# Turning attention probabilities by a DMA transpose of float16 halves instead of PE transposes, from the fifteenth unit on

## The chip, the core and the metric

The kernel runs on one core of one Trainium2 chip. The time is the device time of one execution in microseconds (us). Engines are named as in the profile: PE is TensorE (matmuls), PEld its weight loads, DVE is VectorE, ACT is ScalarE, POOL is GpSimd, SP is SyncE, whose queue issues all of this kernel's DMAs. Each engine runs its instructions in the order in which they stand; an instruction that waits holds everything behind it on the same engine.

## What is computed

Attention inside chunks of 64 positions, then two feed-forward stages. Cut to what matters:

```python
# batch 8, heads 8, sequence 576 in 9 chunks of 64, head size 64
scores = scale * np.matmul(q_c, k_c.transpose(0, 1, 2, 4, 3))
scores = scores - np.max(scores, axis=-1, keepdims=True)
attn = np.exp(scores)
attn = attn / (np.sum(attn, axis=-1, keepdims=True) + 1e-09)
out = np.matmul(attn, v_c)
# then, with x = out as (8, 576, 512):
xn = (x - mu) / np.sqrt(var + 1e-06) * g_ln
x = x + np.maximum(xn @ w_ch1, 0.0) @ w_ch2        # 512 -> 2048 -> 512
# then a gated second stage (moe2) with w_in, a product over the sequence with w_sg, and w_out
```

All of it is float32 in the reference. The kernel forms the large products from float16 halves (a high part and the rest), three matmuls for each.

## The kernel before

The 4608 rows are 36 tiles of 128 rows. `attention(t)`, t from 0 to 35, is one **unit**: one tile, two chunks side by side on the partitions, eight heads. Its steps are scores on PE (`qk`, 16 float32 matmuls of 64x64 into the two banks of `pair`), the row maximum `mx` and the subtraction into `pm` on DVE, the exponential in place on ACT, four 128x128 transposes of `pm` on PE (`pt_`, float32, against `ident`, back into the score half of `pair`), the row sums `sm` and their reciprocals on DVE, a copy of the turned probabilities from `pair` to `pt` on ACT, the product with the values on PE (`pv_`, 16 matmuls of 64x64), and the division into `x` on DVE. From t = 10 (`JOIN`) on, `pv_` of unit t and `qk` of unit t + 1 stand directly behind each other on PE, as one step. `norm` then makes the normalised tile: statistics on DVE, 1/sqrt on POOL, `xn` on DVE, the high half on ACT and the rest on POOL into `hl`, and one DMA transpose `xT<-hl`, issued by SP, of both halves (128 partitions by 1024 float16, eight 128x128 pieces). Two tiles make a block b of 256 rows; `xT` has two buffers, `x` six, `pt` and `pair` one.

The middle of the program is a loop over blocks 4 to 17. For each block and each of eight column groups j, `ff1p` makes 24 matmuls of 256 columns (L677) into a bank, ACT and DVE make sums and halves of it (L692, L699 to L701, L704, L705), and `ff2p`, two groups later, makes 21 matmuls of 256 columns (L729) into `acc`. At the end of a block DVE and ACT bring `acc` back (L752, L757), POOL adds it to x (L762), and SP writes x to `x2d`. Beside this loop run the attention units of the block after next, and, early in it, the preparation of the second stage's weights (`prep`, `halve`: L435, L847, L904 to L910), of which six loads of 1 MB (`raw`, one buffer) are a part. The second stage follows, from a plan of its own.

What sets the order is a planner (`Plan`): every step is entered with an engine, a length in ns, what it reads and writes, a priority and a `lat`, the time that the planner lets pass from the end of the step to the start of a step on another engine that uses it. The planner runs through these lengths and writes out each engine's instructions in the order in which it could start them. Attention units have priority 10 t, the feed-forward steps over 1000, weight preparation 9000 (lower goes first). For t from 12 on, an attention step has `lat` 1000, and two ACT steps have `far`, 3000. So the order is fixed when the program is built; how long a step waits on the chip is another matter.

Of the kernel before, what the change touches and what calls it, by code (L numbers as in the profile page):

```python
# [9 lines left out]
F16 = mybir.dt.float16  # L10
F32 = mybir.dt.float32
# [3 lines left out]
AF = mybir.ActivationFunctionType  # L15
ALU = mybir.AluOpType
# [7 lines left out]
TUNE = dict(  # L24
    a=[-2457, -2682, -1491, -1906, -601, 1801, 3166, 1800],
    w=[2691, 1942, 2717, 1334, 683, 2853, 1967, 684],
    w2=[2022, 3167, 2350, 2598, -1558, -90, 1802, 1496],
    an=[101, 0, 1229, 131, 0, 119, -1201, 1189],
    wb=[112, -57, 0, 128, -102, -1215, 134, -121],
    lo=[0, 0, 0, 0, 1, 0, 0, 1],  # L30
    wl=[0, 0, 1, 1, 0, 0, 1, 0],
    wc=[0, 1, 1, 1, 1, 0, 0, 1],
    wa=[1, 1, 1, 0, 1, 1, 1, 0],
    wm=[0, 0, 0, 1, 0, 1, 1, 0],
    xn=[0, 1, 0, 0, 1, 1, 0, 1],
    g=[150, 12000, 200, 400, 150],
    f=[685, -1559, 2691],
# [105 lines left out]
def fused_kernel(ctx: ExitStack, tc, qkv, w1, w2, g1, w_in, w_out, wsgt, wsgs, g2, b_sg, out):  # L143
    nc = tc.nc
    PSUM = bass.MemoryType.PSUM
    P = 128
# [32 lines left out]
    ident = small.tile([P, P], F32, name="ident")  # L179
# [31 lines left out]
    op = plan.op  # L211
# [59 lines left out]
    def palloc(tag, bufs, shape, dt, pool=None):  # L271
        return plan.buf(tag, bufs, lambda: (pool or pools["att"][1]).tile(shape, dt, tag=tag, name=tag, bufs=bufs))
# [2 lines left out]
    xT_t = {}  # L275
    started = {}
    JOIN = 2 * B0 + 2

    def scores(t, o):

        a = palloc("qk", 2, [P, 2, 512], F32) if t < JOIN else palloc("qkl", 1, [P, 2, 512], F32)
        src = qkv[t].rearrange("p (a f) -> p a f", a=3)
        o("SP", 1700, lambda: nc.sync.dma_start(out=a.t, in_=src[:, 0:2]), wr=[a], lat=2200 if t < JOIN else 4000)
        s2 = pair[t % 2 if t < 6 else 1]

        def qk():
            for hp in range(4):
                for r in (slice(0, 64), slice(64, 128)):
                    for c in range(2):
                        k = hp * 128 + c * 64  # L290
                        nc.tensor.matmul(
                            s2[64 * c:64 * c + 64, r.start // 64, hp * 64:hp * 64 + 64],
                            lhsT=a.t[r, 0, k:k + 64],
                            rhs=a.t[r, 1, k:k + 64],
                            start=True,
                            stop=True,
                        )

        started[t] = a, qk

    def attention(t):
        n = t % 2 if t < 6 else 1
        s2, ks = pair[n], f"pair{n}"
        kp = ks if t < JOIN else "pairv"
        pr = TUNE['a'][t] if t < 8 else 10 * t
        lat = TUNE['g'][2] if t < 8 else 300 if t < JOIN else 600 if t < JOIN + 2 else 1000
        far = dict(lat=1500 if t < JOIN + 2 else 3000) if t >= JOIN else {}
        z = 1

        def o(eng, ns, fn, **k):  # L310
            ns = FAST.get((eng, ns), ns)
            op(eng, ns, fn, prio=k.pop("prio", pr), lat=k.pop("lat", lat), **k)

        if t not in started:
            scores(t, o)
            a, qk = started[t]
            o("PE", 1260 * z, qk, rd=[a], wr=[ks])
        v = palloc("v", 2, [P, 512], F32) if t < JOIN else palloc("vl", 1, [P, 512], F32)
        o("SP", 730, lambda: nc.sync.dma_start(out=v.t, in_=qkv[t].rearrange("p (a f) -> p a f", a=3)[:, 2]), wr=[v], lat=2200)
        mx = palloc("mx", 2, [P, 2, 4, 1], F32)  # L320
        pm = palloc("pm", 2, [P, 4, 2, 64], F32)
        sm = palloc("sm", 2, [P, 4, 2, 1], F32)
        rd = palloc("rd", 2, [P, 4, 2, 1], F32)
        pt = palloc("pt", 1, [P, 4, 128], F32)
        if t < 2:
            x = plan.buf(f"x{t}", 1, lambda: stage.tile([P, 512], F32, name=f"x{t}"))
        else:
            x = palloc("x", 6, [P, 512], F32, px)
        sv = s2[:, :, 0:256].rearrange("p a (h k) -> p a h k", h=4)
        pv = s2[:, :, 256:512].rearrange("p a (h d) -> p a h d", h=4)  # L330

        def pt_():
            for hp in range(4):
                nc.tensor.transpose(
                    s2[:, hp // 2, hp % 2 * 128:hp % 2 * 128 + 128], pm.t[:, hp].rearrange("p a k -> p (a k)"), ident
                )

        def pv_():
            for hp in range(4):
                for r in (slice(0, 64), slice(64, 128)):  # L340
                    for c in range(2):
                        k = c * 256 + hp * 64
                        nc.tensor.matmul(
                            s2[64 * c:64 * c + 64, r.start // 64, 256 + hp * 64:256 + hp * 64 + 64],
                            lhsT=pt.t[r, hp, 64 * c:64 * c + 64],
                            rhs=v.t[r, k:k + 64],
                            start=True,
                            stop=True,
                        )

        def rd_():
            nc.vector.tensor_scalar_add(sm.t, sm.t, 1e-9)
            nc.vector.reciprocal(rd.t, sm.t)

        o("DVE", 600, lambda: nc.vector.tensor_reduce(out=mx.t, in_=sv, axis=AX.X, op=ALU.max), rd=[ks], wr=[mx])
        o("DVE", 600, lambda: nc.vector.tensor_tensor(
            out=pm.t.rearrange("p h a k -> p a h k"), in0=sv, in1=mx.t.to_broadcast([P, 2, 4, 64]), op=ALU.subtract
        ), rd=[ks, mx], wr=[pm])
        o("ACT", 520, lambda: nc.scalar.activation(out=pm.t, in_=pm.t, func=AF.Exp, scale=0.125), wr=[pm], **far)
        o("PE", 850, pt_, rd=[pm, "ident"], wr=[ks, kp] if t >= JOIN else [ks])  # L360
        o("DVE", 600, lambda: nc.vector.tensor_reduce(out=sm.t, in_=pm.t, axis=AX.X, op=ALU.add), rd=[pm], wr=[sm])
        o("DVE", 330, rd_, rd=[sm], wr=[sm, rd])
        o("ACT", 480, lambda: nc.scalar.activation(
            out=pt.t.rearrange("p (a h) q -> p a h q", a=2),
            in_=s2[:, :, 0:256].rearrange("p a (h q) -> p a h q", h=2),
            func=AF.Copy,
        ), rd=[ks], wr=[pt], **far)
        if t < JOIN or t + 1 == NT:
            o("PE", 1260 * z, pv_, rd=[pt, v], wr=[kp])
        else:  # L370
            scores(t + 1, o)
            a_, qk_ = started[t + 1]
            o("PE", 1260, lambda: (pv_(), qk_()), rd=[pt, v, a_], wr=[kp, ks])
        o("DVE", 600, lambda: nc.vector.tensor_tensor(
            out=x.t.rearrange("p (h a d) -> p a h d", h=4, a=2),
            in0=pv,
            in1=rd.t.rearrange("p h a o -> p a h o").to_broadcast([P, 2, 4, 64]),
            op=ALU.mult,
        ), rd=[kp, rd], wr=[x])
        after = pr + (TUNE['an'][t] if t < 8 else 0)  # L380
        norm(t, x, lambda *a, **k: o(*a, prio=after, **k))
# [399 lines left out]

    bW = {"top": Buf("topB", None)}

    ATT = [f"{n}{k}" for n in ("qk", "v", "mx", "pm", "sm", "rd", "bs", "mv", "rs", "hl") for k in range(2)] + ["pt", "xn", "qkl", "vl", "u0", "u1"]
    w2s = {}

    def open_sums():
# [217 lines left out]
    def first_x2():  # L1005
        pr = 9500
        op("DVE", 100, lambda: absmax(redg[:, 0:1], x2mx[:, 0:GT]), rd=[f"x2mx{i}" for i in range(GT)], wr=["redg"], prio=pr, lat=3000)
        par(e2g[:, 0:1], redg[:, 0:1], ["redg"], ["x2e"], pr, True)
        op("DVE", 600, lambda: x2_cols(0, 1), rd=["win_s"], wr=["x2e", "sx0"], prio=pr)
        for p in range(5):  # L1010
            x2_make(plan, 0, p, pr)

    tops = [Buf(f"top{i}", None) for i in range(2)]
    with tc.manual_schedule():
# [10 lines left out]
        for i, b in enumerate(tops):  # L1025
# [4 lines left out]
        op("SP", 60, lambda: nc.sync.dma_start(out=g1s, in_=g1), wr=["g1s"], prio=3, lat=2200)  # L1030
        make_w1(0)
        attention(1)
        make_w1(1)
        attention(2)
# [3 lines left out]
            out=bb, in_=b_sg.rearrange("(o s) -> o s", o=1).partition_broadcast(P)[:, 0, :]  # L1038
# [38 lines left out]
        used += [f"late{n}{b}{k}" for n in "hl" for b in "ab" for k in range(16)]  # L1077
        op(None, 0, open_sums, wr=used + ATT + ["sums"], prio=0)
        for f in range(NF):
# [23 lines left out]
        for b, j in todo:  # L1103
            ff2p(b, j)
        op(None, 0, open_x2, rd=["xsL"], wr=["x2L"] + ATT, prio=0)
        first_x2()
# [19 lines left out]
        def fixed(tag, bufs, shape, dt=F32):  # L1126
            tiles[tag] = [room[-1].tile(shape, dt, name=f"{tag}{k}") for k in range(bufs)]
            return tiles[tag][0]
# [9 lines left out]
        vl = fixed("vl", 1, [P, GT, D], F16)  # L1138
# [459 lines left out]
```

## Time and profile before

| | us |
|---|---|
| median of three runs | 1216.11 |
| lowest and highest run | 1215.26, 1219.31 |
| the profiled execution | 1214.57 |
| its span (first to last instruction) | 1212.80 |

| engine | busy us | share of the span |
|---|---|---|
| PE | 1183.5 | 98% |
| PEld | 885.6 | 73% |
| DVE | 856.5 | 71% |
| ACT | 562.7 | 46% |
| POOL | 299.3 | 25% |

The profile is one execution. Its page gives busy time by engine, the chain of work that ended last, and groups of instructions by line with the idle time before them; the trace behind it answers for single stretches, lines and tiles. Busy time of PE is modelled at its ends, so two matmuls that follow each other overlap in these lists; the distance of two starts says what one costs. What lies around the span is 1214.57 less 1212.80, 1.77 us.

### The profile page before, as it was taken

The numbers are of one execution on the slowest core, as the hardware profiler recorded it, in microseconds if no ns is written. First come the engines' busy times: TensorE is split into PE (matmuls) and PEld (weight loads), VectorE is DVE, ScalarE is ACT, GpSimd is POOL, SyncE is SP. The second block draws the span as 40 slices with busy tenths as digits, with TensorE's granted clock in tenths as the row PEclk, the third lists the DMA queues.
The fourth block names the chain that finished last, engine by engine and source line by source line (L and its number), as shares of the span: only waits on it lengthen the run. The fifth ranks groups of instructions, "written<-read, shape, count | busy, mean of one in ns | idle before, by whom it ended". The sixth has DMA issues, their size and how long they took to land.

```text
span 1212.8 us, 26896 instructions
## 1 busy us (share of the span) xinstructions
PE 1183.5 (98%) x11373; PEld 885.6 (73%) x11373; DVE 856.5 (71%) x1624; ACT 562.7 (46%) x852; POOL 299.3 (25%) x340
## 2 busy tenths in 40 slices
PE   7898999999999999999999999999999999999998
PEld 5677664688888888888888888888456556456453
DVE  7875123899888888667776775767789679568455
ACT  5786410545646674343343334335645435434320
POOL 3842301334312212222221222013302202302200
PEclk8999999999999999999999999999999999999999
DMA  9963002235643221222222111346165472272203
GB/s 293 286 232 88 1 18 55 86 105 151 181 102 69 79 72 62 63 71 62 63 71 71 45 44 19 81 99 161 35 137 153 117 157 90 92 127 70 87 1 113
DMA packets 141528, 118.52 MB, mean 98 GB/s; under 512 B 105440, under 2 KB 114016, under 8 KB 141408
## 3 DMA queue, kind: packets, MB, share of 16 engines
q1 hardware_dynamic: 141408, 116.81, 36.0%
q8 instruction: 89, 1.46, 0.5%
q14 instruction: 31, 0.25, 0.1%
HBM read 72.74 MB, written 18.88 MB: 76 GB/s over the span
## 4 chain that ended last, share of the span: by engine, by line
PE 76%; DVE 13%; DMA 4%; POOL 3%; ACT 2%; issue 2%; another core or an unknown queue 0%; SPq 0%; ACTq 0%; DVEq 0%; POOLq 0%
PE bank L677 19%; PE acc L729 17%; PE pb L1393 5%; PE bank L570 4%; PE pair L591 3%; PE acc L1472 3%; PE pb L1472 3%; PE acc L1393 3%; PE acc L1339 3%; PE pb L1339 3%; PE pb L1297 3%; PE bank L591 2%; PE acc L1297 2%; DVE arena L705 1%; DMA straw<-in_w 1%
## 5 line engine op out<-in xcount | busy, mean ns | idle before, releaser
L677 PE MATMUL bank<-xT,w1h 128*128 128x256 f16 x1792 | 300.6, 273 | 0.0
L729 PEld LDWEIGHTS <-arena 128*128 128x128 f16 x2352 | 228.6, 98 | 30.5 <-issue 1.7
L677 PE MATMUL bank<-xT,w1l 128*128 128x256 f16 x896 | 244.2, 273 | 0.0
L729 PE MATMUL acc<-w,arena 128*128 128x256 f16 x1344 | 202.4, 273 | 1.3 <-ACT arena L704 0.6
L677 PEld LDWEIGHTS <-w1h 128*128 128x128 f16 x1792 | 174.3, 98 | 20.9 <-issue 0.2
L704 ACT ACTIVATE arena<-arena 128x896 f16<-128x896 f32 x112 | 106.1, 948 | 130.5 <-PE acc L729 66.9
L729 PE MATMUL acc<-w2s,arena 128*128 128x256 f16 x1008 | 165.4, 273 | 0.6 <-issue 0.6
L705 DVE TENSOR_TENSOR arena<-arena 128x896 f16<-128x896 f32 x112 | 122.7, 1096 | 48.5 <-ACT arena L704 48.5
L692 ACT ACTIVATE arena<-bank 128x512 f32<-128x512 f32 x112 | 66.3, 592 | 140.7 <-PE bank L677 127.0
L677 PEld LDWEIGHTS <-w1l 128*128 128x128 f16 x896 | 87.7, 98 | 10.1
L570 PE MATMUL bank<-xT,w1h 128*128 128x256 f16 x512 | 85.8, 273 | 7.4 <-DVE latelb L575 3.5
L762 POOL TENSOR_TENSOR x<-x,u 128x256 f32<-128x256 f32 (+1 forms) x60 | 55.7, 955 | 141.2 <-ACT arena L704 97.8
L699 DVE TENSOR_TENSOR arena<-arena 128x256 f32<-128x256 f32 x112 | 55.4, 495 | 40.5 <-ACT arena L692 40.4
L1297 PEld LDWEIGHTS <-x2T 128*128 128x128 f16 x672 | 65.4, 98 | 12.0 <-issue 2.0
L415 POOL TENSOR_TENSOR hl<-xn,hl 128x512 f16<-128x512 f32 x34 | 47.3, 1392 | 104.8 <-ACT hl L413 104.8
L570 PE MATMUL bank<-xT,w1l 128*128 128x256 f16 x256 | 69.8, 273 | 1.2 <-POOL w1l L493 1.2
L401 POOL TENSOR_SCALAR rs<-mv 128x1 f32<-128x1 f32 x36 | 14.6, 404 | 218.4 <-DVE mv L407 217.8
L570 PEld LDWEIGHTS <-w1h 128*128 128x128 f16 x512 | 49.3, 98 | 16.3 <-issue 9.3
L1244 POOL TENSOR_SCALAR rs<-mv 128x2 f32<-128x2 f32 (+1 forms) x20 | 6.2, 311 | 212.2 <-DVE mv L1239 212.0
L700 DVE TENSOR_TENSOR arena<-arena 128x256 f32<-128x256 f32 x112 | 50.3, 449 | 3.8
L1393 PEld LDWEIGHTS <-vh 128*128 128x128 f16 x288 | 28.2, 98 | 33.8 <-issue 0.9
L1393 PE MATMUL pb<-wsg,vh 128*128 128x512 f16 x166 | 51.9, 380 | 0.0
(299 smaller groups left out, 2305.5 us busy)
## 6 DMA issues: line engine op xcount, KB each, us to landing
straw<-in_w SPq DMA_DIRECT2D x16, 1023.8 KB, 7.0
qkl<-in_qkv SPq DMA_DIRECT2D x26, 512.0 KB, 4.1
x2d<-x SPq DMA_DIRECT2D x36, 256.0 KB, 2.0
xr<-x2d SPq DMA_DIRECT2D x36, 256.0 KB, 2.9
out<-xr SPq DMA_DIRECT2D x36, 256.0 KB, 3.1
xs<-x2d SPq DMA_DIRECT2D x27, 256.0 KB, 3.4
vl<-in_qkv SPq DMA_DIRECT2D x26, 256.0 KB, 3.2
qk<-in_qkv SPq DMA_DIRECT2D x10, 512.0 KB, 5.7
```

The source lines that it names most:

```text
L570: nc.tensor.matmul(acc, lhsT=w[j][:, k, fc], rhs=xT.t[:, x, k], start=(n == 0), stop=(n == 11))
L591: nc.tensor.matmul(acc[i], lhsT=h[x].t[:, c], rhs=w2t[j][:, f % 2, y], start=(f == 0 and n == 0), stop=(f == NF - 1 and n == 2),)
L677: nc.tensor.matmul(acc[:, y * 256:y * 256 + 256], lhsT=w[j][:, k, fc], rhs=xT.t[:, x, k], start=(n == 0), stop=(n == 11),)
L692: op("ACT", 500, lambda: nc.scalar.activation(out=o.t[:, 0:4].rearrange("p n t -> p (n t)"), in_=acc, func=AF.Relu, scale=0.5), rd=[kb] + ...
L704: op("ACT", 860, lambda: nc.scalar.activation(out=h.t[:, 0], in_=o.t[:, 1:8], func=AF.Copy), rd=[o] + ar, wr=[h], prio=-100)
L705: op("DVE", 1010, lambda: nc.vector.tensor_tensor(out=h.t[:, 1], in0=o.t[:, 1:8], in1=h.t[:, 0], op=ALU.subtract), rd=[o, h], wr=[h.key + ...
L729: nc.tensor.matmul(acc, lhsT=h.t[:, x, n], rhs=r(y), start=(first and j == 0 and m == 0), stop=(j == 7 and m == 2), skip_group_check=True,)
L762: op("POOL", ns, lambda: nc.gpsimd.tensor_tensor(out=d(), in0=d(), in1=v(), op=ALU.add), rd=u + ["q6", "q5", "q7"], wr=[x], prio=-50, two=1)
L1297: nc.tensor.matmul(ap[:, q * 256:q * 256 + 256], lhsT=xT[:, x, a, k, c], rhs=right(b, 1, k, w), start=(first and n == 0), stop=(k == 1 and ...
L1339: nc.tensor.matmul(ap, lhsT=right(b, 0, k, w)[:, m * 128:m * 128 + 128], rhs=xT[:, x, a, k], start=(first and n == 0), stop=(k == 1 and w ...
L1393: nc.tensor.matmul(ap, lhsT=v[:, fc], rhs=w[:, 0:512], start=(n == 0), stop=end)
L1472: nc.tensor.matmul(ap, lhsT=x[:, k, c], rhs=w[:, k], start=(n == 0), stop=(n == 11))
```

## The change

From unit 14 on (`BYDMA`), `pt_` and the copy from `pair` are gone. In their place ACT copies the exponentials to float16 (`ph`, high half), DVE subtracts that from them (`ph`, low half), SP issues one DMA transpose of both halves (`ptt<-ph`, eight 128x128 float16 pieces, the form of `xT<-hl`), and DVE adds the two turned halves into `pt`. The planner's `lat` for these units goes from 1000 to 400, `far` from 3000 to 1000, and the step behind the new transpose is planned 3500 after its 1100 of issue. From unit 10 on, `pm` has a single buffer of its own (`pml`). `sm` and its reciprocal stay as they were.

```diff
+    BYDMA = 14
...
-        lat = TUNE['g'][2] if t < 8 else 300 if t < JOIN else 600 if t < JOIN + 2 else 1000
-        far = dict(lat=1500 if t < JOIN + 2 else 3000) if t >= JOIN else {}
+        lat = TUNE['g'][2] if t < 8 else 300 if t < JOIN else 600 if t < JOIN + 2 else 1000 if t < BYDMA else 400
+        far = dict(lat=1500 if t < JOIN + 2 else 3000 if t < BYDMA else 1000) if t >= JOIN else {}
...
-        pm = palloc("pm", 2, [P, 4, 2, 64], F32)
+        pm = palloc("pm", 2, [P, 4, 2, 64], F32) if t < JOIN else palloc("pml", 1, [P, 4, 2, 64], F32)
...
-        o("PE", 850, pt_, rd=[pm, "ident"], wr=[ks, kp] if t >= JOIN else [ks])
+        if t < BYDMA:
+            o("PE", 850, pt_, rd=[pm, "ident"], wr=[ks, kp] if t >= JOIN else [ks])
+        else:
+            ph = palloc("ph", 1, [P, 2, 512], F16)
+            ptt = palloc("ptt", 1, [P, 2, 512], F16)
+            flat = lambda: pm.t.rearrange("p h a k -> p (h a k)")
+            o("ACT", 520, lambda: nc.scalar.activation(out=ph.t[:, 0], in_=flat(), func=AF.Copy), rd=[pm], wr=[ph])
+            o("DVE", 600, lambda: nc.vector.tensor_tensor(
+                out=ph.t[:, 1], in0=flat(), in1=ph.t[:, 0], op=ALU.subtract
+            ), rd=[pm], wr=[ph], two=1)
+            o("SP", 1100, lambda: nc.sync.dma_start_transpose(
+                out=ptt.t.rearrange("p x (h q) -> p (x h) q", h=4), in_=ph.t.rearrange("p x f -> p (x f)")
+            ), rd=[ph], wr=[ptt], lat=3500)
+            o("DVE", 600, lambda: nc.vector.tensor_tensor(
+                out=pt.t.rearrange("p h q -> p (h q)"), in0=ptt.t[:, 0], in1=ptt.t[:, 1], op=ALU.add
+            ), rd=[ptt], wr=[pt], two=1, **far)
...
-        o("ACT", 480, lambda: nc.scalar.activation(
+        if t < BYDMA:
+            o("ACT", 480, lambda: nc.scalar.activation(
```

How the order moves is shown at three places. Lines of the new kernel past the change stand 17 lower: L694 is L677 of before, L746 is L729, L722 is L705, L716 to L718 are L699 to L701, L864 is L847, L452 is L435, L377 is L361, L353 and L354 are L352 and L353.

PE before, in the loop, at the end of an `ff1p` (the bank and the halves `w1h`, `w1l` of its weights) where the transposes of unit 17 stand, with the `ff2p` behind them:

```order
L677 LDWEIGHTS w1h_154
L677 MATMUL bank_69<-xT,w1h_154 128x256
L677 LDWEIGHTS w1l_162
L677 MATMUL bank_69<-xT,w1l_162 128x256
L334 MATMUL pair_67<-ident,pm 128x128 x4
L729 LDWEIGHTS arena
L729 MATMUL acc_2746<-w_3_168,arena 128x256
```

The same place on PE now:

```order
L694 LDWEIGHTS w1h_154
L694 MATMUL bank_69<-xT,w1h_154 128x256
L694 LDWEIGHTS w1l_162
L694 MATMUL bank_69<-xT,w1l_162 128x256
L746 LDWEIGHTS arena
L746 MATMUL acc_2746<-w_3_168,arena 128x256
```

Nothing stands between the two groups any more; 22 such rows are gone from PE, and no other row was taken away or added there.

DVE before, unit 17, from its row sums `sm` on (`winT` and `wout` are weight preparation, `arena` the sums and halves of the loop):

```order
L361 TENSOR_REDUCE sm<-pm 128x8
L699 TENSOR_TENSOR arena<-arena 128x2x128
L700 TENSOR_TENSOR arena<-arena 128x2x128
L701 TENSOR_TENSOR arena<-arena 128x128
L352 TENSOR_SCALAR sm<-sm 128x8
L353 RECIPROCAL rd<-sm 128x8
L847 TENSOR_TENSOR winT<-win 128x256
L847 TENSOR_TENSOR winT<-win,winT 128x256
L435 SCALAR_TENSOR_TENSOR wout<-raw,top 128x1024
L705 TENSOR_TENSOR arena<-arena 128x896
```

DVE now, unit 17, from the row behind the new subtraction to the new addition:

```order
L377 TENSOR_REDUCE sm<-pml 128x8
L722 TENSOR_TENSOR arena<-arena 128x896
L353 TENSOR_SCALAR sm<-sm 128x8
L354 RECIPROCAL rd<-sm 128x8
L716 TENSOR_TENSOR arena<-arena 128x2x128
L717 TENSOR_TENSOR arena<-arena 128x2x128
L718 TENSOR_TENSOR arena<-arena 128x128
L864 TENSOR_TENSOR winT<-win 128x256
L864 TENSOR_TENSOR winT<-win,winT 128x256
L452 SCALAR_TENSOR_TENSOR wout<-raw,top 128x1024
L722 TENSOR_TENSOR arena<-arena 128x896
L374 TENSOR_TENSOR pt<-ptt 128x512
```

The addition, on which `pv_` now waits, stands behind eleven rows of other work on DVE.

SP before, late in the loop (`vl` and `qkl` are the loads of the values and of the next unit's queries and keys, `x2d` the writes of finished tiles):

```order
L319 DMA vl<-in_qkv 128x512
L283 DMA qkl<-in_qkv 128x1024
L609 DMA x2d_97<-x 128x512
L609 DMA x2d_98<-x 128x512
L319 DMA vl<-in_qkv 128x512
L283 DMA qkl<-in_qkv 128x1024
L267 DMA_TRANSPOSE xT<-hl 128x8x128 x2
```

SP now, around the same writes:

```order
L320 DMA vl<-in_qkv 128x512
L284 DMA qkl<-in_qkv 128x1024
L626 DMA x2d_97<-x 128x512
L626 DMA x2d_98<-x 128x512
L371 DMA_TRANSPOSE ptt<-ph 128x8x128
L320 DMA vl<-in_qkv 128x512
L284 DMA qkl<-in_qkv 128x1024
L371 DMA_TRANSPOSE ptt<-ph 128x8x128
L267 DMA_TRANSPOSE xT<-hl 128x8x128 x2
```

Each unit has one more issue on SP, behind its loads, and the writes and `xT` transposes keep their places around it.

## Rows read from the trace of the kernel before

**Rows 1.** Page, part 1: engine, busy us, share of the span, instructions.

```profile
PE 1183.5 (98%) x11373; PEld 885.6 (73%) x11373; DVE 856.5 (71%) x1624; ACT 562.7 (46%) x852; POOL 299.3 (25%) x340
```

**Rows 2.** Page, part 4: the chain that ended last, shares by engine.

```profile
PE 76%; DVE 13%; DMA 4%; POOL 3%; ACT 2%; issue 2%; another core or an unknown queue 0%; SPq 0%; ACTq 0%; DVEq 0%; POOLq 0%
```

**Rows 3.** Busy time by stretch of the loop; the first row names the columns.

```profile
core 0: us, PE busy (x) PEld busy (x) DVE busy (x) ACT busy (x) POOL busy (x), PEclk, DMA share, GB/s
287.00:330.00 43.00, 43.00 (x502) 38.27 (x501) 38.67 (x77) 26.61 (x38) 16.41 (x18) 1.00 0.66 193
330.00:372.00 42.00, 41.16 (x536) 36.26 (x534) 35.53 (x71) 22.90 (x40) 7.10 (x8) 1.00 0.56 90
...
415.00:458.00 43.00, 43.00 (x503) 38.38 (x501) 37.76 (x74) 30.05 (x43) 10.34 (x11) 1.00 0.25 65
...
500.00:756.00 256.00, 256.00 (x2899) 227.92 (x2898) 179.22 (x345) 99.16 (x143) 60.68 (x67) 1.00 0.20 55
```

**Rows 4.** Timeline of PE around one unit's transposes: start us, length us, engine, line.

```profile
467.05 0.60 PE L334 MATMUL pair<-ident,pm 128*128 128x128 f32 x4
467.49 0.38 PE L677 MATMUL bank<-xT,w1h 128*128 128x256 f16 x2
```

**Rows 5.** Groups by line and shape: count, busy us, mean ns of one, idle before.

```profile
L334 PE MATMUL pair<-ident,pm 128*128 128x128 f32 x144 | 22.5, 280 | 2.5 <-DVE x L374 1.7 <-ACT pm L359 0.8
...
L413 ACT ACTIVATE hl<-xn 128x512 f16<-128x512 f32 x36 | 22.3, 620 | 35.5 <-DVE xn L410 34.6 <-POOL xn L410 0.9
...
L363 ACT ACTIVATE pt<-pair 128x512 f32<-128x512 f32 x36 | 21.2, 590 | 13.7 <-PE pair L334 13.6
...
L352 DVE TENSOR_SCALAR sm<-sm 128x8 f32<-128x8 f32 x36 | 20.3, 565 | 0.3
...
L410 DVE TENSOR_SCALAR xn<-x,mv,rs 128x512 f32<-128x512 f32 x32 | 17.3, 541 | 1.9 <-POOL rs L404 1.4 <-ACT xn L507 0.5
...
L435 DVE SCALAR_TENSOR_TENSOR win<-raw,top 128x1024 uint32<-128x1024 uint32 x4 | 5.2, 1308 | 1.3 <-ACT top L430 1.3
...
L847 DVE TENSOR_TENSOR winT<-win 128x256 f32<-128x256 f32 x8 | 4.3, 533 | 0.0
```

**Rows 6.** One line, the same subtraction into halves in `norm`, as DVE ran it: ns min/median/max.

```profile
L415 DVE TENSOR_TENSOR hl<-xn,hl x2: 682/704/726, 47.8 to 98.3; 128x512 f16<-128x512 f32 x2
```

**Rows 7.** The existing transposes `xT<-hl`: issue on SP in ns, then time to landing.

```profile
L267 SPq DMA_TRANSPOSE xT<-hl x36: 1231/1237/2533, 21.1 to 743.3; - x36
...
DMA to landing us min/median/max: 3.0/3.5/6.8
```

**Rows 8.** Timeline of PE, the transposes of unit 19, with their wait.

```profile
384.48 0.66 PE L334 MATMUL pair<-ident,pm 128*128 128x128 f32 x4 [1.69 <-DVE x L374]
```

**Rows 9.** Timeline of DVE, two stretches: the loop's sums, and `x` waiting.

```profile
336.37 0.69 DVE L374 TENSOR_TENSOR x<-pair,rd 128x512 f32<-128x512 f32 x1 [3.64 <-remote]
...
376.77 1.08 DVE L705 TENSOR_TENSOR arena<-arena 128x896 f16<-128x896 f32 x1
377.77 0.42 DVE L699 TENSOR_TENSOR arena<-arena 128x256 f32<-128x256 f32 x1
...
378.77 0.68 DVE L214 TENSOR_REDUCE x2mx<-x 128x1 f32<-128x512 f32 x1
379.36 0.42 DVE L699 TENSOR_TENSOR arena<-arena 128x256 f32<-128x256 f32 x1
...
383.73 0.69 DVE L374 TENSOR_TENSOR x<-pair,rd 128x512 f32<-128x512 f32 x1 [2.29 <-DMA x2d<-x]
```

**Rows 10.** The chain that ended last in order of time: one `ff1p` of 24 matmuls.

```profile
717.72 2.62 PE bank L677 x24
```

**Rows 11.** The 1 MB weight loads (L423), time to landing.

```profile
DMA to landing us min/median/max: 4.8/6.2/8.1
```

**Rows 12.** The second stage's transposes (L986, up to fourteen pieces each), time to landing.

```profile
DMA to landing us min/median/max: 2.4/4.1/6.3
```

More of the change, by code (lines that the diff above doesn't have):

```diff
@@ L359, in attention @@
         o("ACT", 520, lambda: nc.scalar.activation(out=pm.t, in_=pm.t, func=AF.Exp, scale=0.125), wr=[pm], **far)
-        o("PE", 850, pt_, rd=[pm, "ident"], wr=[ks, kp] if t >= JOIN else [ks])
+        if t < BYDMA:
[14 more added lines that the diff above has]
+            ), rd=[ptt], wr=[pt], two=1, **far)
         o("DVE", 600, lambda: nc.vector.tensor_reduce(out=sm.t, in_=pm.t, axis=AX.X, op=ALU.add), rd=[pm], wr=[sm])
         o("DVE", 330, rd_, rd=[sm], wr=[sm, rd])
-        o("ACT", 480, lambda: nc.scalar.activation(
[L364 to L367, printed above, removed]
+        if t < BYDMA:
+            o("ACT", 480, lambda: nc.scalar.activation(
+                out=pt.t.rearrange("p (a h) q -> p a h q", a=2),
+                in_=s2[:, :, 0:256].rearrange("p a (h q) -> p a h q", h=2),
+                func=AF.Copy,
+            ), rd=[ks], wr=[pt], **far)
         if t < JOIN or t + 1 == NT:
@@ L782, in fused_kernel @@
     bW = {"top": Buf("topB", None)}
-    ATT = [f"{n}{k}" for n in ("qk", "v", "mx", "pm", "sm", "rd", "bs", "mv", "rs", "hl") for k in range(2)] + ["pt", "xn", "qkl", "vl", "u0", "u1"]
+    ATT = [f"{n}{k}" for n in ("qk", "v", "mx", "pm", "sm", "rd", "bs", "mv", "rs", "hl") for k in range(2)] + ["pt", "xn", "qkl", "vl", "u0", "u1", "pml", "ph", "ptt"]
     w2s = {}
```

## The prediction

> **What bounds the kernel now.** I read the page first: PE is busy 98% of the span [rows 1], and the chain that ended last runs over PE for 76% of it [rows 2]. The second look is by stretch, because an average hides where PE has room. In the loop it has none: 43.00 of 43.00 us from 287 to 330, all 256.00 from 500 to 756, and 41.16 of 42.00 in between [rows 3]. So a PE instruction that goes is time that goes, as long as what PE needs next is there in time. The same rows show who could fail at that: DVE is busy 38.67 of 43 us at the loop's start and 35.53 to 37.76 per window up to 458, then 70% (179.22 of 256). The program order is fixed, so I ask two things of the change: what PE gets back, and whether the longer way from `qk` to `pv_` still fits under the matmuls that stand between them.
>
> **What it removes from PE.** One unit's four transposes start at 467.05 and the next matmul starts at 467.49 [rows 4]: 0.44 us of PE. All 36 units have them (144 in rows 5); 22 lose them. 22 x 0.44 = 9.7 us. Nothing on PE takes their place. There is a second piece: at 384.48 the transposes of unit 19 waited 1.69 us for DVE's `x` of the unit before [rows 8], because they wrote into the bank that `x` reads; that `x` itself waited 2.29 us for a write of a finished tile to land [rows 9]. Without the transposes the first to need that bank is `pv_`, which stood 5 us further on. I count this wait as gone, 1.7 us.
>
> **What it moves on ACT and SP.** ACT loses a copy of 0.59 us and gets one of 0.62 us of the form of L413 [rows 5]: 22 x 0.03 = 0.7 us on an engine busy 46% [rows 1], nothing on the path. SP gets 22 issues of 1.24 us [rows 7]. Behind them stand the next unit's `vl` and `qkl`, needed 13 us later or more, and `xT`, needed a block later; SP is idle most of the time, so I cost this at nothing. If that cover went, each would cost its 1.24 us, 27 us in all. The DMA engines' share is 0.20 late in the loop and 0.66 at its start [rows 3]; the transposes have room except perhaps there. The buffer `pml` is single, but a unit's subtraction comes after everything that reads the last unit's, so it adds no wait.
>
> **What it adds on DVE.** The subtraction is L415's form, which took 0.70 us on DVE [rows 6]. The addition (two float16 in, float32 out) has no row of its own: it can't be dearer than that 0.70, and I take as its lower end the 0.54 of L410 [rows 5], a one-input step of the same size; I take 0.70, since it reads two tensors. Together 1.40 us a unit (1.24 at least), 31 us in all, about 2.8 per 43 us window with two units. The tightest window has 43 - 38.67 = 4.3 us of DVE left, so it fits, but leaves 1.5.
>
> **Whether the chain still fits.** This is where the choice lies. Between `qk` and `pv_` the new order has 126 to 237 matmuls of 256 columns. One costs 2.62 / 24 = 0.109 us [rows 10], so the cover is 13.8 to 25.9 us. Eleven of the 22 units have 13.8 to 16.7 us (units 15, 17, 19, 21, 23, 25, 27, 28, 30, 32, 34); the others have 18.7 or more. Without queues the chain is short: two DVE steps and two ACT steps of 0.6 to 0.7, the subtraction 0.7, 3.5 for the transpose [rows 7], 0.7 for the addition: 7.5 us. What lengthens it is the queue on DVE. I worked out unit 17, whose rows are in the order above. Back to back, a 128x512 step starts 0.60 after the one before (378.77 to 379.36), L705 takes 1.00 and the three sums behind it 1.00 (376.77, 377.77, 378.77) [rows 9]. From the end of `x` of unit 16, which is about the end of `qk` of unit 17, to the end of the subtraction DVE has `mx`, statistics and `pm` (1.8), L705's step (1.0), two `winT` (about 1.0), the sums (1.0), `xn` (0.5) and the subtraction (0.7): 6.0. From there to the end of the addition: row sums (0.6), twice L705's step (2.0), two steps on `sm` (0.57 and under 0.3), the sums (1.0), two `winT` (1.0), `wout` (1.3), the addition (0.7): 7.5 [rows 5, 9]. That is 13.5, against 3.5 for the transpose beside it, so DVE's queue and not the transpose sets the end. The cover is 138 matmuls, 15.1 us: 1.6 us to spare if `x` doesn't wait. In the kernel before, `x` of the unit in front did wait 3.64 us at this place [rows 9]; with that, `pv_` comes 2.0 us late. Unit 15 has the same cover, and DVE must there convert two of the 1 MB loads ahead of its subtraction and its addition; they land in 4.8 to 8.1 us [rows 11], so between 0 and 3 us late; I take 1.5. The other tight units have shorter queues or no such load: 0.5 us in all. New waits: 4.0 us, with bounds 0 and 10 (the last if the 3.64 us wait meets three of the tight units of the loop's busy start). From unit 27 on DVE has 30% of its time free before the change, and I expect no waits.
>
> **The sum**, against the profiled execution: 1214.57 - 9.7 - 1.7 + 4.0 = 1207.2. That execution lies 1.54 under the median of 1216.11, so the forecast for the median is **1208.7 us**, a gain of 0.6%. What is late next is the second stage's start; its last inputs come from the same loop and move with it.
>
> **The transpose's own time.** The existing transposes of the same form landed in 3.0 to 6.8 us [rows 7], and those of up to fourteen pieces in 2.4 to 6.3 [rows 12]. The sum above stands on 3.5. The Trainium skill ("VectorE: DVE Perf Modes", The three transpose paths and Rules for kernel authors) speaks against this change: it gives 390 ns for a 128x128 16-bit transpose on TensorE and 1309 ns by DMA, and says to use TensorE where a PSUM destination will do. Taken one after another, its figure would make the eight pieces 10.5 us; the landings above, 3.5 for eight, do not agree, and four pieces on PE cost 0.44 here and not four times 0.39.
>
> **The rivals.**
> - *All of it comes through.* If DVE reaches the addition in time at units 15 and 17 as well, there are no new waits: 1208.7 - 4.0 = 1204.7. For it speaks that PE stayed full in the window where DVE was at 90% (287 to 330); against it, the 3.64 us.
> - *The busy start eats it.* If waits for tile writes and 1 MB loads meet three or four tight units before DVE thins out, new waits come to 10 us: 1214.7, no measurable change. For it: the DMA share of 0.66 and 0.56 there [rows 3].
> - *DVE becomes the bound, and the kernel is slower.* The added 31 us put DVE's windows up to 458 at 38 to 41 of 43 us; what is ahead of the addition then runs late for the rest of the loop. If each of the eleven tight units waits 1.5 us, 16.5 us: 1208.7 - 4.0 + 16.5 = 1221.2. It decides from 11.4 / 11 = 1.04 us a unit. Against it: DVE is only 70% busy from 500 on, where five of the eleven stand.
> - *The transposes land late.* At three times the row, 10.5 us, the chain of a tight unit is 6.0 + 0.2 + 10.5 + 0.7 = 17.4; over the eleven covers (165.5 us together) that is 11 x 17.4 - 165.5 = 26 us of waits: 1230.7. Only the skill's figure above speaks for it; the slowest landing in rows 7 was 6.8, which still fits.
> - That the change does not do what it says is out: the order has none of the 22 transposes left.
>
> **How the numbers follow.** Chances: forecast 0.50, all of it 0.20, busy start 0.15, DVE as the bound 0.12, late landing 0.03. The measurement tells about 0.3% from no change, 3.6 us, so faster means below 1212.5 and slower above 1219.8. Faster: 0.50 + 0.20 = 0.70; same 0.15; slower 0.15. The range goes from the full gain less the scatter of a run, 1203, to 1218, which takes in the busy start (bound of 10 us of new waits) and part of the third rival; it leaves out the slower cases.
>
> **What would show it.** Right: the 0.44 us slots gone, PE full from 500 to 756, waits of `pv_` for `pt` only before 420 and under 5 us together, landing of `ptt` near 3.5. The second rival shows as waits at units 15 to 21 with DVE held by a DMA; the third as waits for `pt` or for the loop's halves all through the loop, DVE over 90%; the fourth as DVE held by `ptt`. I am wrong above all if the DVE queue of unit 17 is a poor sample of the eleven.

## The result: twice the gain that was forecast, and the profile after

The changed kernel takes **1201.31 us** (1200.75 to 1203.63) against 1215.86 us of the kernel before beside it, a ratio of 0.9878 (95% interval 0.9855 to 0.9901). In a repeat on another chip it took 1200.05 us, a ratio of 0.9882 (0.9869 to 0.9895). That is 14.5 us less, where 7.4 were forecast, and below the range's end of 1203.

The page of the changed kernel, its engines and the chain that ended last (answering to [rows 1, 2]):

```profile
PE 1174.4 (98%) x11285; PEld 877.7 (73%) x11285; DVE 870.7 (72%) x1668; ACT 566.3 (47%) x852; POOL 297.3 (25%) x340
...
PE 88%; DVE 4%; DMA 3%; POOL 2%; ACT 1%; issue 1%; SPq 0%; DVEq 0%; ACTq 0%; POOLq 0%
```

PE lost 88 matmuls, 22 units of four, and 9.1 us of busy time; the chain now runs over PE for 88% of the span instead of 76%. The same stretches as in [rows 3], in the changed kernel:

```profile
core 0: us, PE busy (x) PEld busy (x) DVE busy (x) ACT busy (x) POOL busy (x), PEclk, DMA share, GB/s
287.00:330.00 43.00, 43.00 (x503) 38.25 (x501) 39.76 (x79) 26.43 (x37) 13.97 (x15) 1.00 0.71 189
330.00:372.00 42.00, 42.00 (x494) 37.37 (x492) 38.48 (x80) 22.33 (x33) 11.73 (x14) 1.00 0.47 127
...
415.00:458.00 43.00, 43.00 (x502) 38.28 (x500) 39.51 (x80) 23.62 (x32) 14.02 (x14) 1.00 0.38 89
500.00:756.00 256.00, 256.00 (x2952) 227.31 (x2951) 195.19 (x382) 106.72 (x150) 57.84 (x67) 1.00 0.32 74
```

DVE is fuller in all four (195.19 of 256 us late in the loop, was 179.22), and yet PE waits in none of them, also not from 330 to 372, where it had lost 0.84 us.

All of the gain lies in the loop. Its length can be read from two lines of each kernel, as the start of the first matmul of `ff1p` to the start of the last of `ff2p` (columns: count, ns min/median/max, first and last start in us). Before:

```profile
L677 PE MATMUL bank<-xT,w1h x1792: 271/273/283, 231.4 to 820.2; 128*128 128x256 f16 x200
...
L729 PE MATMUL acc<-w2s,arena x1008: 269/273/283, 240.1 to 827.9; 128*128 128x256 f16 x168
```

and after:

```profile
L694 PE MATMUL bank<-xT,w1h x1792: 272/273/283, 235.4 to 810.2; 128*128 128x256 f16 x200
...
L746 PE MATMUL acc<-w2s,arena x1008: 272/273/283, 244.1 to 817.2; 128*128 128x256 f16 x168
```

827.9 - 231.4 = 596.5 us before, 817.2 - 235.4 = 581.8 after: 14.7 us less. (The loop starts 4.0 us later in this execution of the changed kernel; in its execution on the other chip it starts at 230.4 and is 581.7 long.) 22 slots are 9.7 of that. The other 5.0 us are waits of PE in the loop that are gone. Added up from the starts of PE's instructions they were 5.0 us in seven places: the 1.86 us at 384.48 of [rows 8], and six that the prediction passed over, three of which the timeline of PE before shows like this:

```profile
285.61 0.60 PE L729 MATMUL acc<-w,arena 128*128 128x256 f16 x4 [0.36 <-DVE x L752]
...
377.91 0.28 PE L729 MATMUL acc<-w,arena 128*128 128x256 f16 x1 [0.35 <-DVE arena L705]
...
825.74 0.39 PE L729 MATMUL acc<-w,arena 128*128 128x256 f16 x2 [0.57 <-ACT arena L704]
```

(From start to start they cost 0.52, 0.52 and 0.73; the bracket shows less, because the matmul in front is drawn longer than it holds PE.) The wait at 285.61 and one of 0.20 us just ahead of it, 0.72 together, come and go between executions: they are missing in the kernel with one buffer for `pm` below, which has the order of before, and stand in the one with each transpose issued twice, which has the order of the changed kernel.

The new transposes themselves, by their tile in the changed kernel (answering to [rows 6, 7]):

```profile
L371 SPq DMA_TRANSPOSE ptt<-ph x22: 1232/1232/1263, 299.0 to 696.7; - x22
L374 DVE TENSOR_TENSOR pt<-ptt x22: 678/684/1643, 305.2 to 703.0; 128x512 f32<-128x512 f16 x22
...
DMA to landing us min/median/max: 3.0/3.1/5.7
```

The landing was put at 3.5 and the addition at 0.70; they measured 3.1 and 0.68. DVE never waited for a landing. The 22 subtractions and 22 additions are 31.1 us by their records, as counted, but DVE's busy time rose by only 14.2 us (856.5 to 870.7): its other steps came out 10.7 us shorter in this execution, and the rest is records that overlap. Why the others were shorter was not tried.

### The profile page after: what moved, and what is told of

Its sections match the earlier page's. It is cut to its first block, busy times and chain, and to the rows that moved or that the text cites. A ratio compares the mean times of both kernels' runs of the same rounds, so it can differ in the third digit from the quotient of the medians.

```text
span 1201.4 us, 26816 instructions
## 1 busy us (share of the span) xinstructions
PE 1174.4 (98%) x11285; PEld 877.7 (73%) x11285; DVE 870.7 (72%) x1668; ACT 566.3 (47%) x852; POOL 297.3 (25%) x340
## 4 chain that ended last, share of the span: by engine, by line
PE 88%; DVE 4%; DMA 3%; POOL 2%; ACT 1%; issue 1%; SPq 0%; DVEq 0%; ACTq 0%; POOLq 0%
PE bank L694 24%; PE acc L746 22%; PE pb L1410 5%; PE bank L587 4%; PE acc L1489 3%; PE pair L608 3%; PE bank L608 3%; PE pb L1489 3%; PE acc L1410 3%; PE acc L1356 3%; PE pb L1356 3%; PE pb L1314 3%; PE acc L1314 2%; PE pair L344 1%; DMA straw<-in_w 1%; PE pair L292 1%
## 5 line engine op out<-in xcount | busy, mean ns | idle before, releaser
L694 PE MATMUL bank<-xT,w1h 128*128 128x256 f16 x1792 | 299.7, 273 | 0.0
L746 PEld LDWEIGHTS <-arena 128*128 128x128 f16 x2352 | 228.2, 98 | 27.8 <-issue 0.2
L694 PE MATMUL bank<-xT,w1l 128*128 128x256 f16 x896 | 244.2, 273 | 0.0
L746 PE MATMUL acc<-w,arena 128*128 128x256 f16 x1344 | 202.7, 273 | 0.0
L694 PEld LDWEIGHTS <-w1h 128*128 128x128 f16 x1792 | 175.0, 98 | 20.5
L746 PE MATMUL acc<-w2s,arena 128*128 128x256 f16 x1008 | 165.4, 273 | 0.0
L722 DVE TENSOR_TENSOR arena<-arena 128x896 f16<-128x896 f32 x112 | 122.6, 1096 | 30.0 <-ACT arena L721 29.6
L694 PEld LDWEIGHTS <-w1l 128*128 128x128 f16 x896 | 87.7, 98 | 10.1
L716 DVE TENSOR_TENSOR arena<-arena 128x256 f32<-128x256 f32 x112 | 53.9, 481 | 32.2 <-ACT arena L709 32.0
L432 POOL TENSOR_TENSOR hl<-xn,hl 128x512 f16<-128x512 f32 x34 | 52.3, 1537 | 85.2 <-ACT hl L430 81.9
```

The costliest lines, as they stand in the source:

```text
L694: nc.tensor.matmul(acc[:, y * 256:y * 256 + 256], lhsT=w[j][:, k, fc], rhs=xT.t[:, x, k], start=(n == 0), stop=(n == 11),)
L716: nc.vector.tensor_tensor(out=two(6, 8), in0=two(1, 3), in1=two(0, 2), op=ALU.subtract)
L722: op("DVE", 1010, lambda: nc.vector.tensor_tensor(out=h.t[:, 1], in0=o.t[:, 1:8], in1=h.t[:, 0], op=ALU.subtract), rd=[o, h], wr=[h.key + ...
L746: nc.tensor.matmul(acc, lhsT=h.t[:, x, n], rhs=r(y), start=(first and j == 0 and m == 0), stop=(j == 7 and m == 2), skip_group_check=True,)
```

## The experiments

Loop lengths below are read as above. Each kernel's ratio is to runs of the kernel before on its own chip.

### The planner's numbers without the turn

```diff
-        lat = ... 600 if t < JOIN + 2 else 1000
-        far = dict(lat=1500 if t < JOIN + 2 else 3000) ...
+        lat = ... 600 if t < JOIN + 2 else 1000 if t < 14 else 400
+        far = dict(lat=1500 if t < JOIN + 2 else 3000 if t < 14 else 1000) ...
```

> The kernel before with the planner's new numbers alone: lat 400 and far 1000 from unit 14 on, PE's transposes and ACT's copy kept, pm as before. The changed kernel gained 14.5 us; 22 slots of 0.44 us on PE are 9.7 of them, and about 5 us of waits that PE had in the loop (0.2 to 1.9 us each, seven of them) are gone as well. Theory T (the turn itself frees those waits, since PE no longer has a step between qk and pv_ that can be held up): this kernel keeps them, 1214.5 to 1217 us. Rival P (the new order frees them, whatever turns the probabilities): 5 us less than before, about 1211. Rival N (the smaller lat alone is a loss, because PE's transposes come to stand too early): over 1218, with waits of the transposes for pm.

1211.94 us, ratio 0.9972 (0.9959 to 0.9984): rival P. The loop takes 824.1 - 231.5 = 592.6 us, 3.9 less than before. PE still has its 144 transposes, and yet six of the seven waits are gone. 1.2 us are left: 0.31 of a new one, at a transpose (377.20), and 0.90 from start to start in the third line here, from the timeline of PE:

```profile
L678 PE MATMUL bank<-xT,w1h x1792: 272/273/283, 231.5 to 816.2; 128*128 128x256 f16 x200
...
L730 PE MATMUL acc<-w2s,arena x1008: 272/273/283, 240.1 to 824.1; 128*128 128x256 f16 x168
...
821.90 0.39 PE L730 MATMUL acc<-w,arena 128*128 128x256 f16 x2 [0.73 <-ACT arena L705]
```

So the new order alone takes most of those waits away, with PE's transposes still there (the pair near 285 is in that count, so 3.2 to 3.9 us). From this kernel to the changed one the loop loses 592.6 - 581.8 = 10.8 us: 9.7 of slots and the last 1.2 of waits, within 0.1. The ratios say the same, 0.9972 - 0.9882 is 10.9 us, give or take about 2 us by their intervals. Why each single wait goes with the new order was not tried.

### One buffer for `pm`, alone

```diff
-        pm = palloc("pm", 2, [P, 4, 2, 64], F32)
+        pm = palloc("pm", 2, [P, 4, 2, 64], F32) if t < JOIN else palloc("pml", 1, [P, 4, 2, 64], F32)
```

> The kernel before with the third part of the change alone: one buffer for pm from unit 10 on. The order of every engine is word for word that of before. No theory gives it a gain; if a single buffer held up a step, 0.5 us a unit would be 13 us. Expected: no change, 1214 to 1217 us.

1215.88 us, ratio 1.0001 (0.9985 to 1.0017). The third part alone changes nothing that can be measured. Its loop of 597.6 us has five of the seven waits of before, not the pair near 285, and one place more:

```profile
362.52 0.65 PE L334 MATMUL pair<-ident,pml 128*128 128x128 f32 x4 [1.58 <-ACT pml L359]
```

With the order of every engine unchanged, the sum of these waits is 6.2 us here and was 5.0 before; whether the new place belongs to the single buffer or to this execution was not tried.

### The turn with the planner's old numbers

```diff
-        lat = ... else 1000 if t < BYDMA else 400
-        far = ... else 3000 if t < BYDMA else 1000) ...
+        lat = ... else 1000
+        far = ... else 3000) ...
```

> The changed kernel with the planner's old numbers: lat 1000 and far 3000 in all units from 12 on; halves, DMA transpose and addition as in the changed kernel. Theory T: same as the changed kernel, 1200.5 to 1203 us, with no waits of PE in the loop. Rival P: the 5 us of waits come back, about 1206. Both keep the 9.7 us of the slots.

1268.0 us, ratio 1.0435 (1.0415 to 1.0455): both theories missed by more than 60 us. The group of `ff1p` on the page has the first piece (busy us, mean ns, then idle before it), and the timeline of PE the second, the start of the next stage:

```profile
L694 PE MATMUL bank<-xT,w1h 128*128 128x256 f16 x1792 | 308.4, 278 | 28.0 <-DMA xT<-hl 28.0
```

```profile
404.57 0.39 PE L694 MATMUL bank<-xT,w1h 128*128 128x256 f16 x2 [4.62 <-DMA xT<-hl]
...
883.54 0.80 PE L1314 MATMUL pb<-win,x2T 128*128 128x256 f16 x3 [22.52 <-ACT o L1220]
```

28.0 + 22.5 = 50.5 us of waits for attention's results, none of which either of the two kernels has, out of 67 us lost by the ratio to the changed kernel. In the loop (624.9 us, 43.1 longer) all waits of PE come to 34.1 from start to start, and the other 9.0 are matmuls at a lower granted clock behind the longer waits (last section). The attention had fallen behind. Its pace is read from `pv_`, 26 units from unit 10 to unit 35; here with the old numbers, then in the changed kernel:

```profile
L344 PE MATMUL pair<-vl,pt x832: 218/218/267, 229.5 to 800.2; 64*64 64x64 f32 x167
```

```profile
L344 PE MATMUL pair<-vl,pt x832: 218/218/267, 234.3 to 716.1; 64*64 64x64 f32 x167
```

(800.2 - 229.5) / 25 = 22.8 us a unit against (716.1 - 234.3) / 25 = 19.3. The loop needs a unit every half block, 581.8 / 28 = 20.8 us. The kernel before had 20.0, by its own rows of `pv_`. The planner adds `lat` to each step of the turn, of which there are more than before, and thinks a unit longer than it is; the order it writes then holds `pv_` back on PE although `pt` is ready (the addition ended 1.7 to 5.5 us before `pv_` from unit 14 on). That is theory Q of the next two.

> The changed kernel with lat 1000 (the old number) and far 1000 (the new one). With both old numbers it took 1268 us. Theory Q: what cost 66 us there is that the planner, which adds lat and far to every step between engines, could place a unit only every 22.8 us or so, more than half a block of the loop; the attention fell behind, and PE waited in each block for xT and 22.7 us at the start of the second stage. In this order the last pv_ stands 695 us of PE work into the program (674 in the changed kernel, 722 with both old numbers) and two units fit in a block (covers of 16.6 and 23.8 us in turn), so Q says no waits for xT: 1201 to 1207 us. Rival: lat 1000 costs by itself, on every one of eight steps of a unit; then a good part of the 66 us stays, over 1230 us.

> The changed kernel with lat 400 (the new number) and far 3000 (the old one). The last pv_ stands at 724 us of PE work, as with both old numbers. Theory Q: the two far steps of a unit (exponential and addition) are what makes the planned unit too long, so this one is as slow, 1255 to 1275 us, with waits for xT in each block and a late second stage. Rival (lat costs, far is neutral): 1201 to 1207 us.

Old `lat` and new `far` (1000 and 1000): 1212.76 us, ratio 0.9983 (0.9974 to 0.9991). Its pace is 20.1 us a unit (230.5 to 733.2), its loop 581.8 us, as the changed kernel's, without a wait. So far Q is right; but the result is 6 us outside what Q expected, because the second stage starts late, which Q had not looked at:

```profile
827.73 1.65 PE L1314 MATMUL pb<-win,x2T 128*128 128x256 f16 x7 [8.86 <-ACT o L1220]
```

New `lat` and old `far` (400 and 3000): 1249.37 us, ratio 1.0284 (1.0264 to 1.0305), a little less slow than expected. Pace 22.2 us a unit (231.8 to 786.4), and both kinds of wait:

```profile
456.21 0.59 PE L694 MATMUL bank<-xT,w1h 128*128 128x256 f16 x2 [11.18 <-DMA xT<-hl]
...
865.71 1.65 PE L1314 MATMUL pb<-win,x2T 128*128 128x256 f16 x7 [22.47 <-ACT o L1220]
```

`far` of the two steps is what makes the loop wait; `lat` at 1000 leaves the loop alone, but sets the last `pv_` 21 us later in the loop and costs 9 us of waiting at the stage's start and about 2 more behind it, where the granted clock was 0.50 (827 to 832). Smaller numbers still bring nothing:

> The changed kernel with smaller numbers still for the planner from unit 14 on: lat 200 and far 500 (400 and 1000 in the changed kernel). The covers of the tight units shrink to 12.4 to 15.6 us (14.3 to 17.3 in the same count for the changed kernel). If smaller numbers are better as such, it is under 1199. If the changed kernel's 1.2 us before pv_ are a cushion that lat and far put there, and PE is full with it, nothing can be gained and the shorter covers cost the tight units 0 to 1 us each: 1200 to 1206 us.

1201.91 us, ratio 0.9882 (0.9863 to 0.9901), the changed kernel's time. PE was all but full (1.2 us of waits, 0.72 of them the pair near 285), so there was nothing left to gain.

### How much is spare: the landing and the addition

The same order of all engines, with each new transpose issued twice in a row, or each addition done two or three times in place.

```diff
+            for _ in range(2):
                 nc.sync.dma_start_transpose(out=ptt..., in_=ph...)
...
+            for _ in range(k):          # k = 2 or 3
                 nc.vector.tensor_tensor(out=pt..., in0=ptt.t[:, 0], in1=ptt.t[:, 1], op=ALU.add)
```

> The changed kernel with each of the 22 new DMA transposes issued twice, one after the other (the second waits on SP until the first has landed); the order of all engines is otherwise the changed kernel's. The first landed 3.1 us after its issue. If DVE's queue and not the landing sets when the addition runs, most of the second landing is hidden: by the measured slack of each unit (time from issue to addition, and from addition to pv_), 0.4 us in all, 1201.7 us; 20 us, about 1221, if a landing takes 4.3 us counted with its issue. If the transposes are on the path, each costs its 3.1 us: 22 x 3.1 = 68 us, about 1270.

1205.34 us, ratio 0.9916 (0.9901 to 0.993), 4 us over the changed kernel: ten times the first estimate, but a long way from 20 or 68. By the tile `ptt`:

```profile
  DMA ptt<-ph: 13.8, 12
...
  PE pair L344: 2.9, 4
...
DMA to landing us min/median/max: 3.0/3.2/4.8
```

Twelve additions on DVE now waited for a landing, 13.8 us in all, and of that four waits reached PE (2.9 us). With one transpose the landing is hidden behind DVE's queue in all 22 units of the changed kernel: each addition starts 0.8 us or more after its own landing.

> The changed kernel with each of the 22 additions done twice, in place, in the changed kernel's order: 0.72 us of DVE more a unit (one addition more, as the three-fold one, 1.45 us more, showed them). The three-fold one lost 13.6 us. Theory M (a unit's DVE chain has about 1.2 us to spare before pv_, and only what goes beyond it is paid): 0.5 to 1.5 us over the changed kernel, 1200.5 to 1202 us. Rival (DVE has nothing to spare; the loss is in proportion): 13.6 x 0.72 / 1.45 = 6.8 us, about 1207.

> The changed kernel with each of the 22 additions done three times over, in place; the order is otherwise the changed kernel's. Two more additions back to back are 1.2 to 1.4 us of DVE a unit. If the measured slack between the addition's end and pv_ (0.25 to 2.15 us, 1.2 in the middle, 11.9 in two units) is all that counts, 1.7 to 3.9 us more than the changed kernel, 1203 to 1205 us. If the change left DVE at its limit, so that every microsecond more is paid, 22 x 1.3 = 28 us more, about 1230 us.

One addition more (0.72 us a unit): 1202.62 us, ratio 0.9893 (0.9874 to 0.9913), 1 to 3 us over the changed kernel by medians and ratios, about as theory M said (its loop is 583.0 us, 1.2 longer). Two more (1.45 us a unit): 1213.63 us, ratio 0.9992 (0.998 to 1.0005), 13.6 us over the changed kernel beside it on the same chip: the 3.9 of the first theory was far too low there. The waits of PE, first with one more, then with two more (us in total, times, longest):

```profile
PE pair L344 <- DVE pt L376: 0.9, 2, 0.5
```

```profile
PE pair L344 <- DVE pt L376: 9.9, 16, 1.9
...
PE acc L750 <- DVE arena L726: 1.0, 2, 0.5
```

Measured in the changed kernel, the addition ends 0.9 to 2.2 us before `pv_` in 19 of the 22 units (0.25 in one, 11.9 in two). With 1.45 us more, 16 of the 22 additions are late. The loss is more than the sum of what each unit lacked, and a late DVE is late with the next unit's steps too; that this is the reason was not tried. With 1.45 us more a unit nearly all of the gain is gone.

### More units

```diff
-    BYDMA = 14
+    BYDMA = 10      # and 12
```

> The changed kernel with the turn from unit 10 on in place of 14: four more units lose their 0.44 us slots. If a slot on PE is worth its length wherever PE is full, 4 x 0.44 = 1.8 us less: 1199.5 us. If the busy start of the loop (DVE near 90%, the 1 MB loads) can't take the longer way, the four units wait: no gain or a loss of 1 to 2 us each, 1201 to 1208 us.

> The changed kernel with the turn from unit 12 on, two units more than in the changed kernel and two less than from unit 10 on, which lost 10 us of waits in two places (5.3 us of pv_ for its addition behind weight preparation on DVE, 3.9 us for halves of the sums). If those waits belong to units 10 and 11 alone, two slots are gained: 0.9 us under the changed kernel, 1199.2. If every unit of the loop's busy start meets the weight preparation, 2 to 6 us more than the changed kernel, 1202 to 1206. The covers of units 14 and 15 are 10.4 and 14.3 us here, which speaks for the second.

From unit 10: 1211.72 us, ratio 0.9978 (0.9968 to 0.9987). From unit 12: 1210.52 us, ratio 0.9956 (0.9939 to 0.9972). Both lose to the changed kernel, by 12 and 9 us by the ratios, four and two slots fewer on PE notwithstanding; both are more than the second theory allowed. From unit 10, on PE:

```profile
270.65 0.60 PE L344 MATMUL pair<-vl,pt 64*64 64x64 f32 x12 [5.11 <-DVE pt L374]
...
301.31 0.39 PE L746 MATMUL acc<-w,arena 128*128 128x256 f16 x1 [3.70 <-DVE arena L722]
```

and on DVE just ahead of the first of these, weight preparation (L652) and then the addition:

```profile
268.49 0.37 DVE L652 TENSOR_TENSOR tf<-bf 128x256 f32<-128x256 f32 x1
268.90 0.43 DVE L652 TENSOR_TENSOR tf<-bf,tf 128x256 f32<-128x256 f32 x1
...
269.91 0.68 DVE L374 TENSOR_TENSOR pt<-ptt 128x512 f32<-128x512 f16 x1
```

DVE is busy without a break up to that addition and waits for no DMA, and PE has only 71 matmuls (7.8 us) between this unit's `qk` and its `pv_`, for a chain of 13.0 us. So it is a busy start like the prediction's rival, at a unit that the change left alone, but what holds DVE is its queue and not a load or a write. From unit 12, PE waits 1.2, 3.7 and 2.7 us (at 265.04, 289.86 and 302.96), the first for an addition, the others for ACT's and DVE's sums.

## Why the prediction was wrong

- **Slots, 9.7 us: right.** From the planner's numbers alone to the whole change the loop lost 10.8 us, 9.7 and the 1.2 of waits that were left.
- **The wait at 384.48, 1.7 us: right that it goes, but only a third of what goes.** The step took it that this wait goes with PE's transposes, and counted this one alone. All seven waits went, 5.0 us, and 3.9 us of the loop with the new `lat` and `far` while PE still had its transposes, this wait among them; so the reason given was not needed. The prediction had no term for these numbers at all: it read the new order for the turn's new waits, and not for the old waits that the same order would take away. That is 3.3 us.
- **New waits, 4.0 us: this step failed, there were none.** Unit 17's chain was worked out as 13.5 us; `qk` ended at 346.84 and the addition at 360.84, 14.0. But the 2.0 us came from adding the 3.64 us that `x` had waited in [rows 9], and that wait belonged to the old order: the second execution of it, with one buffer for `pm`, has it again (3.8 us), and the kernel with the planner's numbers alone has not. In the timeline of DVE after, `x` of unit 16 starts 0.35 us after `qk`, and the addition has no bracket either:

```profile
347.19 0.68 DVE L391 TENSOR_TENSOR x<-pair,rd 128x512 f32<-128x512 f32 x1
...
359.15 1.08 DVE L722 TENSOR_TENSOR arena<-arena 128x896 f16<-128x896 f32 x1
360.15 0.69 DVE L374 TENSOR_TENSOR pt<-ptt 128x512 f32<-128x512 f16 x1
```

  It ends 1.1 us before `pv_`. Unit 15, put at 1.5 us for a late load, had 1.4 us to spare. The cover (15.1 us for both, counted and measured) and the queue were right; the extra waits were carried over from a trace whose order no longer held.
- **The sum.** 9.7 + 5.0 - 0 = 14.7 in place of 9.7 + 1.7 - 4.0 = 7.4. The range's lower end was the sum without new waits less a run's scatter, and had no room for old waits that go.
- **The rivals.** *All of it comes through* was the mechanism, 3.3 us short. *The busy start* did not come; what came near it shows with the turn from unit 10 or 12 on. *DVE as the bound* needed waits of 1.04 us in each tight unit and there were none; but 0.72 us more of DVE a unit cost 1 to 3 us and 1.45 cost 13.6, so the changed kernel lies within 1.5 us of DVE a unit of losing its gain. *Late landing* is out. The Trainium skill ("VectorE: DVE Perf Modes", The three transpose paths) gives 1309 ns by DMA for a 128x128 16-bit piece; eight times that would be 10.5 us, an estimate from the page's figure, and the trace does not agree, for the eight pieces here landed in 3.1 us from the issue. Even two transposes in a row cost 4 us in all. The Trainium skill's rule (same page, Rules for kernel authors) to use TensorE where a PSUM destination will do does not pay here: PE was full and the DMA path hidden, and leaving TensorE took 10.8 us off the loop.
- **What no rival saw:** that the turn with the old planner numbers is 53 us slower than before. The `lat` and `far` lines were described as part of the change and then costed at nothing.

## What to carry to other kernels

A line in a diff that only changes a planner's numbers is a change of its own: cost it by the order that it makes, for the waits it takes away as well as for those it adds, and don't carry a wait from the old trace into a new order. In a loop where one engine is full, what it waits for must come at a pace that fits: divide the distance from the first to the last unit by the steps between them, and compare with what the loop needs (19.3 against 20.8 us here, and 22.8 in the order that lost). Moving work from a full engine pays its full length as long as the engine that takes it has room in each unit; here 0.72 us more a unit cost 1 to 3 us in all, and 1.45 us nearly the whole gain.

## What the runs showed of the hardware that was not expected

Some waits of PE cost more than their length, because the granted clock is down after them. In the kernel with the turn from unit 10 on, by stretch around its two waits:

```profile
core 0: us, PE busy (x) PEld busy (x) DVE busy (x) ACT busy (x) POOL busy (x), PEclk, DMA share, GB/s
260.00:265.00 5.00, 5.00 (x48) 4.49 (x47) 4.92 (x10) 2.81 (x4) 1.95 (x2) 1.00 0.14 56
265.30:270.60 5.30, 0.24 (x3) 0.00 (x0) 5.20 (x13) 1.69 (x3) 1.33 (x1) 0.97 0.52 98
270.70:273.00 2.30, 2.30 (x67) 2.06 (x68) 1.33 (x2) 1.43 (x3) 2.05 (x1) 0.50 0.11 15
...
301.30:304.00 2.70, 2.69 (x13) 1.94 (x14) 2.63 (x7) 1.18 (x2) 0.00 (x0) 0.50 0.66 189
```

After 5.3 us almost without work, and again after 3.8 us, the granted clock was 0.50 (1.2 GHz) for the 2.3 and 2.7 us that followed, while PE was busy all the time: 13 matmuls of 256 columns in 2.7 us, where at 1.00 it does about 25. So each of these waits cost one to one and a half us more than the wait. Not every wait does that. In the turn with the planner's old numbers the granted clock was 0.50 to 0.59 for about 3 us behind five waits of PE for `xT` in the loop (3.5 to 4.6 us by their brackets), and 1.00 right behind those of 1.7 us (at 542.26) and 3.2 us (at 451.30). The waits of under 2 us in the kernel before did not show it either: its granted clock was 1.00 in the stretch from 330 to 420 us, which has four of them.
